# Two attentions in one kernel: the main loop's order and PSUM banks as one written list

## The chip, the core and the metric

The kernel runs on one core of a Trainium2 chip. The metric is the device time of the core in microseconds: 1790.12 us, the median of three runs (1788.89 to 1790.79). The engines that matter are TensorE (PE; its weight loads are shown as PEld), VectorE (DVE), ScalarE (ACT), GpSimd (POOL) and the DMA queue of SyncE (SP). Each engine runs its own instructions strictly in the order in which they stand, and waits where an operand is not ready.

## What is computed

Two multi-head attentions over 2048 rows of width 640 with 32 heads of 20 columns, in fp32; their outputs stand side by side.

```python
def _A_ref(x, wqkv, wo):            # local, dilated: 8 keys, 2 apart
    qkv = (x @ wqkv).reshape(B, S, 3, H, Dh).transpose(2, 0, 3, 1, 4)
    ...
    logits = jnp.einsum("bhsd,bhswd->bhsw", q, kg) * scale
    attn = _softmax(jnp.where(mask, logits, -1e9), axis=-1)
    o = jnp.einsum("bhsw,bhswd->bhsd", attn, vg)
    return o.transpose(0, 2, 1, 3).reshape(B, S, D) @ wo
def _B_ref(x, wqkv, wo):            # full attention
    scores = jnp.einsum("bhqd,bhkd->bhqk", q, k) * (Dh ** -0.5)
    o = jnp.einsum("bhqk,bhkd->bhqd", _softmax(scores), v)
    return o.transpose(0, 2, 1, 3).reshape(B, S, D) @ wo
return jnp.concatenate([a, b], axis=-1)
```

## The kernel before

Up to about 440 us the kernel projects q, k and v of both attentions. Then comes **the loop** over 512 steps of attention B. A step takes one block of 128 keys for one chunk of 512 queries and one group of four heads; 16 steps make a unit (one chunk), 64 a group. The last 24 steps run after the loop in a part of their own, which the change leaves alone, and then the rest of B's output projection follows.

Each step has three kinds of work for PE, and every product goes to a PSUM bank (there are eight, of 128 x 512 fp32) from which another engine must read it before PE may write there again:

- **S**, the scores: four halves, each one matmul `ps_st<-bq,bk` into one bank, read by one exp on ACT (`e<-ps_st`).
- **M**, the row maxima that a later step's exp needs: the scores of a block 24 steps ahead (`LEAD`) are made once more, four halves of one matmul `ps_st<-bk,bq` each, and DVE reads each with a maximum over its 512 columns (`mx<-ps_st`). Two halves in neighbouring banks can be read by one reduction of 1024 columns.
- **V**, the product of the exps of two steps ago (`LAG`) with the values: four matmuls `ps_st<-e,vb` side by side into one bank, which is kept over two steps, then copied out by ACT (`more<-ps_st`) and added up by POOL (`braw<-braw,more`).

The matmuls of one pair of halves run side by side in the array. In the same loop the rest of attention A runs: its scores and values on POOL (`akv`, `al`, `ao`), its softmax's maximum and reciprocal on DVE, and, for each of 16 tiles of 128 rows, five transposes on DVE (`turn<-ao`), a trip through DRAM, a split on POOL (`aot`) and two **out pieces** of 15 matmuls each on PE (`ps_st<-ww,aot`, `a_out`, line 480), each copied out by ACT (`ro<-ps_st`).

The order of all this is the order in which the Python code issues it: the wrapper `InOrder` (lines 48 to 62) records every instruction and keeps it there, so in the profile nearly all of them have line 61, and one goes by tile names. Two strings of letters set the loop's order (lines 984 and 985):

```python
PLAIN = "VYMSVYMSYY"
MIXED = "VYMSVYjMYYFYMSYVYMSVYSMYVYkYSVMSY"
```

V begins a step (`begin`, line 960, which also issues the DMAs, the POOL work and the short DVE jobs that are due) and issues the V product of two steps before. S is a pair of score halves, M a pair of maximum halves in two neighbouring banks with one reduction of 1024, Y one score half and one maximum half, whose reduction is one of 512. F is one out piece. j and k run short DVE jobs that wait in two lists, transposes among them (j: one softmax job or else three transposes; k: one softmax job and five transposes). MIXED is taken when an out piece is about to be ready, PLAIN otherwise.

The banks are reckoned while the code issues: `read_at` holds for each bank when it will have been read, by clocks that `InOrder` and `b_two` (line 779) keep for PE, ACT and DVE with fixed prices, and `one` and `two` (lines 139 and 145) take the bank, or the two neighbouring banks, that come free first.

Of the kernel before, what the change touches and what calls it, by code (L numbers as in the profile page):

```python
# [21 lines left out]
KC = 5  # L22
# [25 lines left out]
class InOrder:  # L48


    def __init__(self, tc, engine, fixed=0.0, rate=math.inf):
        self.tc, self.engine, self.fixed, self.rate = tc, engine, fixed, rate
        self.us = 0.0

    def __getattr__(self, name):
        op = getattr(self.engine, name)

        def emit(*a, us=None, **k):
            n = max([math.prod(x.shape[1:]) for x in a if hasattr(x, "shape")], default=0)
            self.us += self.fixed + n / self.rate if us is None else us  # L60
            return self.tc.keep_in_program_order(op(*a, **k))  # L61
        return emit


@with_exitstack
def attention_pair(ctx, tc, xa, wqk_a, wv_a, wo_a, xb, wqk_b, wv_b, wo_b, oa, ob):
# [5 lines left out]
    dr = ctx.enter_context(tc.tile_pool(name="dr", bufs=1, space=bass.MemoryType.DRAM))  # L72
    pe, gp, sp = (InOrder(tc, e) for e in (nc.tensor, nc.gpsimd, nc.sync))
    dve, act = InOrder(tc, nc.vector, 0.064, 960), InOrder(tc, nc.scalar, 0.111, 1400)

# [4 lines left out]
    def after(n, fn, *args):  # L80
        due.setdefault(now[0] + n, []).append((fn, args))

    loop = [None]

# [26 lines left out]
    taken = {}  # L111
    read_at = []

    def bank():

        if read_at:
            n = one(pe.us)
            pe.us = max(pe.us, read_at[n]) + 2.2
            act.us = max(act.us, pe.us + 0.05)
        else:  # L120
            n = free.pop(0)
        t = psb[:, n]
        taken[id(t)] = (n, t)
        return t

    def give(t):

        n = taken.pop(id(t))[0]
        if read_at:
            read_at[n] = act.us + 0.2  # L130
        else:
# [12 lines left out]

    def two(t):

        return min(range(7), key=lambda n: (max(t, read_at[n], read_at[n + 1]), abs(read_at[n] - read_at[n + 1])))

# [231 lines left out]
    def a_softmax(t):  # L380

        _, L, _ = a_t[t]
        if t % (NT // 2) == 0:
            pool(L, L, mask, ALU.add)
        yield
        if t < NT - 1:
            yield
        m = sb.tile([128, 4, H], F32, tag="am", bufs=2, name="am")
        job(soft_jobs, 0, lambda: dve.tensor_reduce(m[:, 0], L.rearrange("p o h -> p h o"), AX.X, ALU.max, us=0.53))
# [11 lines left out]
        job(soft_jobs, 0, lambda: dve.reciprocal(m[:, 0], m[:, 0], us=0.23))  # L401
        yield
        pool(L, L, m[:, 0].unsqueeze(1).to_broadcast([128, WIN, H]), ALU.mult)
# [210 lines left out]
    def max_rows(m4, m1, q, qc):  # L614
# [5 lines left out]
        def turn():  # L620

            dve.transpose(raw, m1, us=0.135)

# [19 lines left out]
    def normalize(raw, g, c0, t, gap, then):  # L643
# [15 lines left out]
        t = odd(t + gap)  # L659
        after(t, lambda: dve.reciprocal(sm, sm, us=0.157))  # L660
        after(t + 1, sp.dma_start, s_d[1].rearrange("j (p c) -> j p c", c=16), sm)
# [74 lines left out]

    exp_at = {}
    behind_v = [False]

    def b_pv(i):  # L740
        u, kb = divmod(i, NKB)
        g, qc = divmod(u, NQC)
        n, part = divmod(kb, 2)
        if read_at:
            t = max(pe.us + 0.12, exp_at.pop(i))
            if part == 0:
                o = one(t)
                accs[u] = o, psb[:, o]
                t = max(t, read_at[o])
                read_at[o] = 1e9  # L750
            pe.us = t + 0.866
            behind_v[0] = True
        elif part == 0:
            accs[u] = None, bank()
        o, acc = accs[u]
        for j in range(GH):
# [5 lines left out]
        del accs[u]  # L762
        act.us = max(act.us, pe.us + 0.322)
# [7 lines left out]
        if o is None:  # L771
            give(acc)
        else:
            read_at[o] = act.us + 0.25
        if kb == NKB - 1:
            last = g == NG - 1
            normalize(raws.pop(u), g, qc * 512, *((2, 3) if last else (5, 6)), (lambda: out_last(qc)) if last else None)

    def b_two(what):

        t = pe.us + 0.129 * behind_v[0]
        lag = 0.53 if behind_v[0] else 0.44
        both = what[0][0] == what[1][0] == "m"
        if both:
            n = two(t)
            ns, ts = (n, n + 1), [max(t, read_at[n], read_at[n + 1])] * 2
        else:
            ns, ts = [], []
            for _ in range(2):
                ns.append(one(max([t] + ts), *ns))  # L790
                ts.append(max([t] + ts + [read_at[ns[-1]]]))
        pe.us = ts[1] + (0.236 if ts[1] > ts[0] + 0.05 or (ts[0] < t + 0.02 and not behind_v[0]) else 0.336)
        behind_v[0] = False
        for (kind, *at), n in zip(what, ns):
            (s_matmul if kind == "s" else m_matmul)(*at, psb[:, n])
        for (kind, i, j, r), n, t in zip(what, ns, ts):
            if kind == "s":
                act.us = max(act.us, t + lag)
                s_exp(i, j, r, psb[:, n])
                exp_at[i] = act.us + 0.2  # L800
                read_at[n] = act.us + 0.18
            elif not both or r == 1:
                pq, ch = divmod(i % NKB, 2)
                m4 = mxt[i // NKB][0]
                dve.us = max(dve.us, t + lag)
                if both:
                    dve.tensor_reduce(m4[:, :, pq, 2 * ch + j], psb[:, ns[0]:ns[0] + 2], AX.X, ALU.max)
                    read_at[ns[0]] = dve.us + 0.13
                else:
                    dve.tensor_reduce(m4[:, r, pq, 2 * ch + j:2 * ch + j + 1], psb[:, n], AX.X, ALU.max)  # L810
                read_at[n] = dve.us + 0.13

    s_next, m_next, m_open, m_half = [0], [0], [None], set()

# [13 lines left out]
    def m_done(m):  # L828

        if m[1] in m_half:  # L830
            max_end(m[1])
        m_half.symmetric_difference_update({m[1]})

    def b_token(kind):

        m = None
        if kind == "S":
            what = [s_half(), s_half()]
        elif kind == "M":
            m = m_two()  # L840
            what = [(*m, 0), (*m, 1)]
        else:
# [7 lines left out]
        b_two(what)  # L850
        if m:
            m_done(m)
# [102 lines left out]
    loop[0] = now[0] + 1  # L955
    read_at += 8 * [0.0]
    for e in (pe, act, dve):
        e.us = 0.0

# [23 lines left out]

    PLAIN = "VYMSVYMSYY"
    MIXED = "VYMSVYjMYYFYMSYVYMSVYSMYVYkYSVMSY"
    i, order, mixed = 0, "", 0
    while i < NS - LEAD or order:
        if not order:
            if not left_a[0] and not WO_b:
                load_out(wo_b, WO_b)  # L990
            order = PLAIN
            if i + 6 <= NS - LEAD and ready_a and ready_a[0][0] <= now[0] + 3 and (
                    soft_jobs or next_a[0] == len(UNITS) or now[0] > max(mixed, ready_a[0][0]) + 14):
                order, mixed = MIXED, now[0] + 6
        kind, order = order[0], order[1:]
        if kind == "F":
            out_piece()
        elif kind == "j":
            run_jobs(*((soft_jobs, 1) if soft_jobs else (turn_jobs, 3)))
        elif kind == "k":  # L1000
            run_jobs(soft_jobs, 1)
            run_jobs(turn_jobs, KC)
        elif kind != "V":
            b_token(kind)
        else:
            begin(i)
# [9 lines left out]

    read_at.clear()
    for i in range(NS - LEAD, NS + LAG):
# [65 lines left out]
```

## Time and profile before

| what | us |
|---|---|
| median of three runs | 1790.12 (1788.89 to 1790.79) |
| span of the profiled execution | 1787.0 |
| median less that span | 3.1 |
| first exp of the loop starts | 440.0 |
| last maximum of the loop starts | 1669.6 |
| last exp starts | 1735.9 |

The profile is of one execution; its own time outside the span is not shown, so the span is set beside the median. The page gives each engine's busy time; a busy PE is one with a matmul in flight, not one at its full rate. Views by stretch ("windows") give the same for any part of the span, and a timeline gives the instructions in order, with the idle time of the engine before each in square brackets and what ended it. DVE and ACT overlap the end of one instruction with the start of the next, so in a run of equal instructions the busy time of the group divided by its count is less than the mean length of one.

### The profile page before, as it was taken

The numbers are of one execution on the slowest core, as the hardware profiler recorded it, in microseconds if no ns is written. First come the engines' busy times: TensorE is split into PE (matmuls) and PEld (weight loads), VectorE is DVE, ScalarE is ACT, GpSimd is POOL, SyncE is SP. The second block draws the span as 40 slices with busy tenths as digits, with TensorE's granted clock in tenths as the row PEclk, the third lists the DMA queues.
The fourth block names the chain that finished last, engine by engine and source line by source line (L and its number), as shares of the span: only waits on it lengthen the run. The fifth ranks groups of instructions, "written<-read, shape, count | busy, mean of one in ns | idle before, by whom it ended". The sixth has DMA issues, their size and how long they took to land. (4 is left out here: it accounts for less than half of the span.)

```text
span 1787.0 us, 31655 instructions
## 1 busy us (share of the span) xinstructions
PE 1772.1 (99%) x11211; PEld 987.1 (55%) x11211; DVE 1340.0 (75%) x1834; ACT 1327.2 (74%) x2593; POOL 1217.1 (68%) x1072
## 2 busy tenths in 40 slices
PE   9999999999999999999999999999999999999999
PEld 7988888887344444444444444444444434443469
DVE  3100232367999999999999999999999999999300
ACT  4222322222998999999999999998998998899881
POOL 0000069226679999989998999999999997337241
PEclk9999999999999999999999999999999999999999
DMA  6333696854535444354536336354444453113123
GB/s 228 116 100 102 190 304 245 270 187 139 152 88 148 124 136 120 106 151 133 147 99 170 96 113 163 121 159 130 133 142 124 122 149 94 30 44 86 32 70 114
DMA packets 191191, 240.22 MB, mean 134 GB/s; under 512 B 89020, under 2 KB 115260, under 8 KB 190040
## 3 DMA queue, kind: packets, MB, share of 16 engines
q1 hardware_dynamic: 190456, 237.54, 44.5%
q8 instruction: 88, 1.44, 0.4%
q14 instruction: 71, 0.58, 0.1%
q10 hardware_dynamic: 576, 0.66, 0.1%
HBM read 173.21 MB, written 64.91 MB: 133 GB/s over the span
## 5 line engine op out<-in xcount | busy, mean ns | idle before, releaser
L61 DVE TENSOR_REDUCE mx<-ps_st 128x1 f32<-128x512 f32 (+1 forms) x1512 | 1218.2, 871 | 57.7 <-PE ps_st L61 51.3
L61 ACT ACTIVATE e<-ps_st 128x512 f32<-128x512 f32 x2048 | 1066.2, 615 | 37.7 <-PE ps_st L61 16.4
L61 PE MATMUL ps_st<-bq,bk 62*128 62x512 f32 x2048 | 614.4, 436 | 1.4 <-DVE mx L61 0.6
L61 PE MATMUL ps_st<-bk,bq 60*128 60x512 f32 x2048 | 593.4, 446 | 3.9 <-DVE mx L61 2.1
L61 PEld LDWEIGHTS ps_st<-bq,bk 62*128 62x128 f32 x2048 | 283.0, 184 | 479.3 <-ACT e L61 282.3
L61 PE MATMUL ps_st<-e,vb 128*32 128x512 f32 x4096 | 543.7, 605 | 3.8 <-ACT e L61 2.6
L61 POOL TENSOR_TENSOR braw<-braw,more 128x512 f32<-128x512 f32 x224 | 287.8, 1285 | 136.5 <-ACT more L61 133.2
L61 POOL TENSOR_TENSOR akv<-akv,aq 128x1280 f32<-128x1280 f32 x64 | 189.0, 2953 | 234.4 <-DMA akv<-ka_d 234.4
L61 PEld LDWEIGHTS ps_st<-bk,bq 60*128 60x128 f32 x2048 | 267.7, 184 | 71.3 <-DVE mx L61 36.7
L61 POOL TENSOR_TENSOR akv<-akv 128x640 f32<-128x640 f32 (+3 forms) x304 | 282.2, 928 | 23.8
L61 ACT COPY ro<-ps_st 128x320 f32<-128x320 f32 (+2 forms) x124 | 61.2, 495 | 226.6 <-PE ps_st L61 177.2
L61 PEld LDWEIGHTS ps_st<-e,vb 128*32 128x32 f32 x4096 | 82.1, 108 | 158.8 <-ACT e L61 76.6
L61 POOL TENSOR_TENSOR akv<-akv,al 128x1280 f32<-128x1280 f32 x64 | 152.0, 2375 | 0.2
L61 ACT COPY more<-ps_st 128x512 f32<-128x512 f32 x224 | 133.4, 595 | 2.9 <-PE ps_st L61 2.7
L61 PE MATMUL ps_st<-wc,xn 128*128 128x512 f32 (+1 forms) x576 | 133.5, 376 | 0.4 <-ACT xn L61 0.4
L61 PE MATMUL ps_st<-ww,xn 128*128 128x320 f32 x768 | 125.8, 314 | 0.0
L61 PEld LDWEIGHTS ps_st<-ww,xn 128*128 128x128 f32 x768 | 113.4, 188 | 20.1 <-ACT ve L61 7.7
L61 PEld LDWEIGHTS ps_st<-wc,xn 128*128 128x128 f32 x576 | 106.2, 188 | 18.4 <-ACT xn L61 1.0
L61 PE MATMUL ps_st<-xn,w 128*128 128x512 f32 x480 | 115.7, 390 | 0.0
L61 PEld LDWEIGHTS ps_st<-xn,w 128*128 128x128 f32 x480 | 90.1, 188 | 19.4
L61 ACT CAST pr<-ps_st 128x512 fp32r<-128x512 f32 x40 | 23.5, 587 | 101.0 <-PE ps_st L61 101.0
L61 DVE TENSOR_TENSOR pr<-ps_st,pr 128x512 fp32r<-128x512 f32 x40 | 27.7, 692 | 91.7 <-ACT pr L61 91.7
(64 smaller groups left out, 986.0 us busy)
## 6 DMA issues: line engine op xcount, KB each, us to landing
akv<-ka_d SPq DMA_DIRECT2D x128, 320.0 KB
akv<-va_d SPq DMA_DIRECT2D x128, 320.0 KB
kb_d<-pr SPq DMA_DIRECT2D x20, 512.0 KB
qb_d<-pr SPq DMA_DIRECT2D x20, 512.0 KB
bk<-kb_d SPq DMA_DIRECT2D x16, 640.0 KB
bq<-qb_d SPq DMA_DIRECT2D x64, 160.0 KB
rb<-s_d SPq DMA_DIRECT2D x128, 64.0 KB
stg<-xb SPq DMA_DIRECT2D x12, 512.0 KB
```

The costliest lines, as they stand in the source:

```text
L61: return self.tc.keep_in_program_order(op(*a, **k))
```

## The change

Both strings, the clocks, `read_at`, `one` and `two` go. In their place stands `ORDER`, one string of some 6200 characters that lists every token of the loop, with the bank or banks that it writes. The letters mean what they meant, with these differences:

- V is followed by the bank that its product takes at every second step. F is followed by the bank of the out piece.
- S and Y are followed by two banks. M has one bank, the first of two neighbours, and one reduction of 1024.
- **N** is new: a pair of maximum halves in two banks of any place, read by two reductions of 512.
- j runs one transpose; k is gone. Softmax jobs run at the starts of steps only, as `begin` did before too.

The list holds 488 V, 32 F, 660 S, 632 Y, 509 M, 151 N and 80 j. The two strings came, over the loop, to 488 V, 32 F, 488 S, 976 Y and 488 M. The work is the same: 1952 score halves, 1952 maximum halves, 488 V products, 32 out pieces, 80 transposes. What moves is the order on PE, DVE and ACT, which bank each pair takes, and which maximum halves share a reduction. `m_done` now counts the halves of a unit, because halves of different steps can be open at once.

```diff
@@ InOrder
-    def __init__(self, tc, engine, fixed=0.0, rate=math.inf):
-        self.tc, self.engine, self.fixed, self.rate = tc, engine, fixed, rate
-        self.us = 0.0
+    def __init__(self, tc, engine):
+        self.tc, self.engine = tc, engine
...
+        return lambda *a, **k: self.tc.keep_in_program_order(op(*a, **k))
@@ bank, give
-        if read_at:
-            n = one(pe.us)
-            pe.us = max(pe.us, read_at[n]) + 2.2
-            act.us = max(act.us, pe.us + 0.05)
-        else:
-            n = free.pop(0)
+        n = given.pop(0) if given else free.pop(0)
...
-    def one(t, *but):
-
-        at = [1e9] + read_at + [1e9]
-        return min((n for n in range(8) if n not in but), key=lambda n: (
-            max(t, read_at[n]), -max(t, at[n]) - max(t, at[n + 2])))
...
@@ b_two
-    def b_two(what):
...
+    def b_two(what, ns, one):
+
         for (kind, *at), n in zip(what, ns):
             (s_matmul if kind == "s" else m_matmul)(*at, psb[:, n])
-        for (kind, i, j, r), n, t in zip(what, ns, ts):
+        for (kind, i, j, r), n in zip(what, ns):
             if kind == "s":
                 s_exp(i, j, r, psb[:, n])
-            elif not both or r == 1:
+            elif not one or r == 1:
...
+                if one:
+                    dve.tensor_reduce(m4[:, :, pq, 2 * ch + j], psb[:, n - 1:n + 1], AX.X, ALU.max)
                 else:
                     dve.tensor_reduce(m4[:, r, pq, 2 * ch + j:2 * ch + j + 1], psb[:, n], AX.X, ALU.max)
@@ the loop
-    PLAIN = "VYMSVYMSYY"
-    MIXED = "VYMSVYjMYYFYMSYVYMSVYSMYVYkYSVMSY"
-    i, order, mixed = 0, "", 0
-    while i < NS - LEAD or order:
...
+    ORDER = (
+        "Y07M1S36M4V0Y71M4M2S06V7Y06M2S14Y75V0Y16M2S74VY71M5S42S03N17V4Y05S61M2VY07M5S13S42N70V1Y36M4S72VY07M2S64S51N70"
...
+    for kind, *ns in re.findall("[A-Zj][0-7]*", ORDER):
+        ns = [int(n) for n in ns]
+        if kind == "j":
+            run_jobs(turn_jobs, 1)
+        elif kind not in "FV":
+            b_token(kind, ns)
+        else:
+            given += ns
+            if kind == "F":
+                out_piece()
+                continue
...
```

How the instructions move, at two places. First PE around the 13th out piece, where `bq,bk` is a score half, `bk,bq` a maximum half, `e,vb` a V product and `ww,aot` the piece. Before:

```order
L61 MATMUL ps_st<-bq,bk 128x512 x2
L61 MATMUL ps_st<-e,vb 32x512 x4
L61 MATMUL ps_st<-bq,bk 128x512
L61 MATMUL ps_st<-bk,bq 128x512 x3
L61 MATMUL ps_st<-bq,bk 128x512
L61 MATMUL ps_st<-bk,bq 128x512
L61 MATMUL ps_st<-bq,bk 128x512
L61 MATMUL ps_st<-bk,bq 128x512
L61 MATMUL ps_st<-ww,aot 128x320 x15
L61 MATMUL ps_st<-bq,bk 128x512
```

and now:

```order
L56 MATMUL ps_st<-e,vb 32x512 x4
L56 MATMUL ps_st<-bq,bk 128x512
L56 MATMUL ps_st<-bk,bq 128x512 x5
L56 MATMUL ps_st<-bq,bk 128x512 x2
L56 MATMUL ps_st<-ww,aot 128x320 x15
L56 MATMUL ps_st<-bq,bk 128x512
L56 MATMUL ps_st<-bk,bq 128x512 x3
L56 MATMUL ps_st<-bq,bk 128x512 x3
```

Before, the piece stood behind V, Y, M, Y, Y, so that the last two maximum halves before it came one by one, each beside a score half. Now it stands behind V, Y, M, M, S: the maximum halves come first, four of them in two neighbouring pairs, and the pair right before the piece is one of scores. The piece itself stands some 16 steps earlier in the loop than its counterpart did.

Second, DVE around the transposes of the seventh tile of A, where `mx<-ps_st 128x2` is a reduction of 1024 and `128x1` one of 512. Before:

```order
L61 TENSOR_REDUCE mx_8420<-ps_st 128x2
L61 TENSOR_REDUCE mx_8420<-ps_st 128x1
L61 TENSOR_REDUCE mx_8420<-ps_st 128x2
L61 TENSOR_REDUCE mx_8420<-ps_st 128x1 x2
L61 STREAM_TRANSPOSE turn<-ao 128x128 x5
L61 TENSOR_REDUCE mx_8420<-ps_st 128x1
L61 TENSOR_REDUCE mx_8420<-ps_st 128x2
L61 TENSOR_REDUCE mx_8420<-ps_st 128x1 x2
```

and now:

```order
L56 STREAM_TRANSPOSE turn<-ao 128x128
L56 TENSOR_REDUCE mx_7976<-ps_st 128x1
L56 TENSOR_REDUCE mx_7976<-ps_st 128x2
L56 TENSOR_REDUCE mx_8423<-ps_st 128x1 x5
L56 TENSOR_REDUCE mx_2486<-mx_7976 128x16
L56 STREAM_TRANSPOSE mtr<-mx_2486 128x32
L56 TENSOR_REDUCE mx_8423<-ps_st 128x2
L56 STREAM_TRANSPOSE turn<-ao 128x128
L56 TENSOR_REDUCE mx_8423<-ps_st 128x1
L56 STREAM_TRANSPOSE turn<-ao 128x128 x3
L56 TENSOR_REDUCE mx_8423<-ps_st 128x1
L56 TENSOR_REDUCE mx_8423<-ps_st 128x2
```

Before, the five transposes of a tile stood together, 16 steps behind the place where POOL's last addition to the tile is issued; now they are spread, the first 6 steps behind that place and the last 8. The five reductions of 512 in a row are those of N and Y tokens that follow each other.

More of the change, by code (lines that the diff above doesn't have):

```diff
@@ L1 @@
-import math
+import re
 from contextlib import ExitStack
@@ L48 @@
 class InOrder:
-    def __init__(self, tc, engine, fixed=0.0, rate=math.inf):
-        self.tc, self.engine, self.fixed, self.rate = tc, engine, fixed, rate
-        self.us = 0.0
+    def __init__(self, tc, engine):
+        self.tc, self.engine = tc, engine
     def __getattr__(self, name):
         op = getattr(self.engine, name)
[L58 to L62, printed above, removed]
+        return lambda *a, **k: self.tc.keep_in_program_order(op(*a, **k))
 @with_exitstack
@@ L72, in attention_pair @@
     dr = ctx.enter_context(tc.tile_pool(name="dr", bufs=1, space=bass.MemoryType.DRAM))
-    pe, gp, sp = (InOrder(tc, e) for e in (nc.tensor, nc.gpsimd, nc.sync))
-    dve, act = InOrder(tc, nc.vector, 0.064, 960), InOrder(tc, nc.scalar, 0.111, 1400)
+    pe, dve, act, gp, sp = (InOrder(tc, e) for e in (nc.tensor, nc.vector, nc.scalar, nc.gpsimd, nc.sync))
     now = [0]
@@ L81, in after @@
         due.setdefault(now[0] + n, []).append((fn, args))
-    loop = [None]
+    loop = [None, False]
     def odd(n):
@@ L111, in attention_pair @@
     taken = {}
-    read_at = []
+    given = []
     def bank():
-        if read_at:
-            n = one(pe.us)
-            pe.us = max(pe.us, read_at[n]) + 2.2
-            act.us = max(act.us, pe.us + 0.05)
-        else:
-            n = free.pop(0)
+        n = given.pop(0) if given else free.pop(0)
         t = psb[:, n]
-        taken[id(t)] = (n, t)
+        taken[id(t)] = (None if loop[0] is not None and loop[1] else n, t)
         return t
@@ L128, in give @@
         n = taken.pop(id(t))[0]
-        if read_at:
-            read_at[n] = act.us + 0.2
-        else:
+        if n is not None:
             free.append(n)
@@ L400, in a_softmax @@
         yield
-        job(soft_jobs, 0, lambda: dve.reciprocal(m[:, 0], m[:, 0], us=0.23))
+        job(soft_jobs, 0, lambda: dve.reciprocal(m[:, 0], m[:, 0]))
         yield
@@ L620, in turn @@
         def turn():
-            dve.transpose(raw, m1, us=0.135)
+            dve.transpose(raw, m1)
         def parts():
@@ L659, in normalize @@
         t = odd(t + gap)
-        after(t, lambda: dve.reciprocal(sm, sm, us=0.157))
+        after(t, dve.reciprocal, sm, sm)
         after(t + 1, sp.dma_start, s_d[1].rearrange("j (p c) -> j p c", c=16), sm)
@@ L743, in b_pv @@
         n, part = divmod(kb, 2)
[L744 to L755, printed above, removed]
+        if part == 0:
+            accs[u] = bank()
+        acc = accs[u]
         for j in range(GH):
@@ L770, in b_pv @@
             after(1, pool, raws[u], raws[u], more, ALU.add)
[L771 to L774, printed above, removed]
+        give(acc)
         if kb == NKB - 1:
@@ L777, in b_pv @@
             normalize(raws.pop(u), g, qc * 512, *((2, 3) if last else (5, 6)), (lambda: out_last(qc)) if last else None)
-    def b_two(what):
[L781 to L793, printed above, removed]
+    def b_two(what, ns, one):
         for (kind, *at), n in zip(what, ns):
             (s_matmul if kind == "s" else m_matmul)(*at, psb[:, n])
-        for (kind, i, j, r), n, t in zip(what, ns, ts):
+        for (kind, i, j, r), n in zip(what, ns):
             if kind == "s":
-                act.us = max(act.us, t + lag)
                 s_exp(i, j, r, psb[:, n])
-                exp_at[i] = act.us + 0.2
-                read_at[n] = act.us + 0.18
-            elif not both or r == 1:
+            elif not one or r == 1:
                 pq, ch = divmod(i % NKB, 2)
                 m4 = mxt[i // NKB][0]
[L805 to L808, printed above, removed]
+                if one:
+                    dve.tensor_reduce(m4[:, :, pq, 2 * ch + j], psb[:, n - 1:n + 1], AX.X, ALU.max)
                 else:
                     dve.tensor_reduce(m4[:, r, pq, 2 * ch + j:2 * ch + j + 1], psb[:, n], AX.X, ALU.max)
-                read_at[n] = dve.us + 0.13
-    s_next, m_next, m_open, m_half = [0], [0], [None], set()
+    s_next, m_next, m_open, m_left = [0], [0], [None], {}
     def s_half():
@@ L828, in m_done, with b_token @@
     def m_done(m):
[L830 to L834, printed above, removed]
+        u = m[1] // NKB
+        m_left[u] = m_left.get(u, 2 * (NKB - (LEAD % NKB if u == LEAD // NKB else 0))) - 1
+        if m_left[u] == 0:
+            max_end(u * NKB + NKB - 1)
+    def b_token(kind, ns):
         m = None
@@ L838, in b_token @@
             what = [s_half(), s_half()]
[L839 to L842, printed above, removed]
+        elif kind == "Y":
             o = s_half()
@@ L849, in b_token @@
                 what = [o, (*m, 1 - o[3])]
-        b_two(what)
+        else:
+            m = m_two()
+            what = [(*m, 0), (*m, 1)]
+        b_two(what, ns if len(ns) == 2 else (ns[0], ns[0] + 1), kind == "M")
         if m:
@@ L955, in attention_pair @@
     loop[0] = now[0] + 1
-    read_at += 8 * [0.0]
-    for e in (pe, act, dve):
-        e.us = 0.0
+    loop[1] = True
     def begin(i):
@@ L989, in attention_pair @@
+    i = 0
+    for kind, *ns in re.findall("[A-Zj][0-7]*", ORDER):
[4 more added lines that the diff above has]
+            b_token(kind, ns)
+        else:
+            given += ns
+            if kind == "F":
+                out_piece()
+                continue
             if not left_a[0] and not WO_b:
                 load_out(wo_b, WO_b)
[L991 to L1005, printed above, removed]
             begin(i)
@@ L1015, in attention_pair @@
             i += 1
-    read_at.clear()
+    loop[1] = False
     for i in range(NS - LEAD, NS + LAG):
```

65 lines of the change are left out of this document (58 added, 7 removed).

## The prediction

> **What bounds the kernel now.** I read the page first, then busy times by stretch, then who waits for whom, then one place in the timeline.
>
> ```profile
> PE 1772.1 (99%) x11211; PEld 987.1 (55%) x11211; DVE 1340.0 (75%) x1834; ACT 1327.2 (74%) x2593; POOL 1217.1 (68%) x1072
> L61 ACT ACTIVATE e<-ps_st x2048: 589/605/708, 440.0 to 1735.9; 128x512 f32<-128x512 f32 x187
> L61 DVE TENSOR_REDUCE mx<-ps_st x1512: 626/691/1241, 366.5 to 1669.6; 128x1 f32<-128x512 f32 x158, 128x2 f32<-128x1024 f32 x31
> ```
>
> The first line is of the page, the other two of the views by tile (count, shortest/median/longest in ns, first and last start). The page points to PE, at 99%. But the loop is what the change touches: from the first exp at 440.0 to the last maximum at 1669.6, some 1230 us. In that stretch (columns: length, then PE, PEld, DVE, ACT, POOL busy, then clock, DMA share and GB/s):
>
> ```profile
> 440.00:1670.00 1230.00, 1221.52 (x8288) 532.46 (x8284) 1195.79 (x1663) 1139.19 (x2244) 1060.08 (x921) 1.00 0.42 120
> ```
>
> DVE is busy 1195.8 of 1230 us, 97%, and ACT 93%. PE's 99% is no limit: its weight loads tell what it really does, which is to stand before banks that have not been read yet (waits from 475 to 1635 us):
>
> ```profile
> PEld ps_st L61 <- ACT e L61: 352.1, 609, 1.0
> PEld ps_st L61 <- DVE mx L61: 176.6, 356, 1.0
> ```
>
> That is 528.7 of 1160 us. So in the loop PE is paced by its readers, and DVE has the least room. The chain that ended last agrees: it runs through the maxima at the loop's end, and only then through PE for the last 24 steps and the projection, which the change does not touch:
>
> ```profile
> 1633.33 18.68 DVE mx L61 x24
> 1669.91 113.64 PE ps_st L61 x777
> ```
>
> What a better order can win is thus DVE's idle time in the loop, 1230 - 1195.8 = 34.2 us, and whatever changes in DVE's own work. Where does it sit idle? Busy time of DVE alone, in stretches chosen by the out pieces:
>
> ```profile
> 661.00:689.00 28.00, 27.96 (x39) 1.00 0.42 128
> 689.00:741.00 52.00, 50.14 (x72) 1.00 0.48 137
> 741.00:755.00 14.00, 13.96 (x21) 1.00 0.04 7
> 840.00:892.00 52.00, 50.33 (x73) 1.00 0.50 147
> 1500.00:1600.00 100.00, 99.88 (x694) 47.38 (x686) 92.62 (x129) 88.42 (x175) 35.18 (x34) 1.00 0.18 43
> ```
>
> Under PLAIN (first and third line) DVE is full: 27.96 of 28 and 13.96 of 14 us. Each stretch of two MIXED patterns with their two out pieces loses 1.86 and 1.67 us. There are 16 such pairs of pieces; 13 at about 1.77 make 23.0 us, and the last three lie in the last line, where DVE (third busy time) is idle for 7.4 us. Together 30.4 of the 34.2 us. One piece close up (timeline, columns: start, length, instruction, idle before it):
>
> ```profile
> 692.08 2.43 PE L61 MATMUL ps_st<-ww,aot 128*128 128x320 f32 x15
> 692.11 2.35 DVE L61 TENSOR_REDUCE mx<-ps_st 128x2 f32<-128x1024 f32 x3
> 694.44 0.50 PE L61 MATMUL ps_st<-bq,bk 62*128 62x512 f32 x1
> 694.54 0.42 ACT L61 COPY ro<-ps_st 128x320 f32<-128x320 f32 x1 [1.62 <-PE ps_st L61]
> 695.01 6.00 DVE L61 TENSOR_REDUCE mx<-ps_st 128x1 f32<-128x512 f32 x7 [0.55 <-PE ps_st L61]
> ```
>
> The piece holds PE for 694.44 - 692.08 = 2.36 us, and the first maximum fed after it starts 695.01 - 694.44 = 0.57 us after its matmul. DVE had work for 2.35 us when the piece began and then stood for 0.55. To lose nothing it must have 2.9 us in its queue at a piece.
>
> **The change part by part.** *DVE's own work.* The reductions by shape:
>
> ```profile
> L61 DVE TENSOR_REDUCE mx<-ps_st 128x2 f32<-128x1024 f32 x536 | 649.9, 1216 | 33.0 <-PE ps_st L61 32.8
> L61 DVE TENSOR_REDUCE mx<-ps_st 128x1 f32<-128x512 f32 x976 | 632.7, 681 | 24.7 <-PE ps_st L61 18.4
> ```
>
> Busy time over count is 1.212 us for a double and 0.648 for a single one. The list has 509 doubles for 488 and 632 + 2 x 151 = 934 singles for 976: +21 x 1.212 - 42 x 0.648 = -1.8 us. On the bound, so all of it counts.
>
> [...]
>
> *The out pieces.* From the order of both kernels I counted, for each of the 32 pieces, what DVE has to do between the last reduction whose bank PE must take back before the piece and the first reduction fed after it, at 1.212 and 0.648 us and the rows' times for short jobs. That is the most its queue can hold. Before, 24 of 32 pieces have 2.51 to 3.12 us (mean of all 3.13), so any wait of PE for ACT on the way leaves less than 2.9. In the list 28 have more than 3.2 us, the mean is 3.57, and one (2.94) is near the limit; 0.44 us more per piece. With 0.55 us at the piece above I put what all 32 lose now at 16 us, and let 2 remain: -14 us.
>
> *The rest of the mixed stretches.* 30.4 - 16 = 14.4 us are idle there away from the pieces, behind V products that follow too few maximum halves, as in MIXED's "kYSVMSY". The list has no fixed pattern there and orders each place by itself; since I cannot see how each turns out, I take half: -7 us, with 0 and -14 as bounds.
>
> *Overlap.* A single reduction shows 681 ns by itself but 648 in the group's busy time, so one that follows its predecessor at once hides part of itself. Some 60 waits (the next line) end with a reduction that does not. Without most of them: -2 us, bounds 0 and -5.
>
> ```profile
> DVE mx L61 <- PE ps_st L61: 26.1, 59, 1.5
> ```
>
> *What costs nothing.* Clocks and bank choice are Python; no instruction is in them. Out pieces stand up to 30 steps earlier, ACT's copy and the store with them; the exps around hide them as now. The same 80 transposes are spread one by one; same busy time.
>
> Sum: -1.8 - 14 - 7 - 2 = -24.8, say -25 us. Span 1787.0 - 25 = 1762; with the 3.1 us by which the median lies above the span, **1765 us**. Bounds of the unknown terms, everything working together: -1.8 - 34.2 - 5 = -41 (1749); only the pieces: -16 (1774).
>
> What binds next at -25 us? ACT has 91 us of room. POOL is nearer, since A's work fills it until about 1500 us:
>
> ```profile
> 600.00:1500.00 900.00, 894.88 (x6074) 390.48 (x6074) 877.44 (x1227) 834.24 (x1644) 853.70 (x736) 1.00 0.46 132
> ```
>
> Its 853.7 of 900 us leave 46 us; of the 25 some 18 fall into this stretch, so POOL goes to 97%, not over.
>
> **Rivals.**
>
> *Everything closes up.* DVE never starves, span 1746, median 1749. For it: PLAIN stretches do run full. Against: 488 V products and 32 pieces would all have to fit.
>
> *The idle time moves.* The list packs maximum halves ahead of pieces, so the tokens beside have fewer, and DVE loses under the plain steps what it gains at pieces; within 3.6 us of now, **1790**. For it: PLAIN's 99.9% has nothing to give and any new pattern there can only lose. Against: the count of queued work rises at the pieces without a like fall elsewhere.
>
> *Banks that fit the list's clock and not the chip's.* PE stands in order, so a bank that is read late holds everything behind it, the feed of DVE included. A maximum half that takes back a bank from DVE itself is safe only if DVE has more to do than the 0.57 us from matmul to reduction, and behind a V product more than that product too:
>
> ```profile
> 695.62 1.06 PE L61 MATMUL ps_st<-e,vb 128*32 128x512 f32 x8
> 696.62 0.50 PE L61 MATMUL ps_st<-bq,bk 62*128 62x512 f32 x1
> ```
>
> That is 1.00 us, 1.57 together. By the order, halves with at most 1.25 us of DVE work in between go from 146 to 270. If the 124 more stand behind V products or waits for ACT and lose 0.3 us each, 37 us, the sum turns to +12: **1802**. It decides once the mean loss exceeds 25/124 = 0.2 us. For it: the 528.7 us of waits above show that PE arrives late at banks as a rule. Against: most of those 124 need no V in between, and 0.65 us then cover 0.57.
>
> *Transposes too early.* They stand 5 to 9 steps (once 2) behind POOL's last addition instead of mostly 16; should POOL fall further behind than 5 steps (12 us at 2.4 us a step), DVE, the bound, waits for it at each of the 16 tiles. At 95 to 97% load POOL's queue can grow. Two to three us each would be +40, with the sum +15: **1805**. In the stretch above an addition to `braw` runs about 5 us behind the copy that feeds it, which leaves 7:
>
> ```profile
> 690.86 0.59 ACT L61 COPY more<-ps_st 128x512 f32<-128x512 f32 x1
> 696.09 1.28 POOL L61 TENSOR_TENSOR braw<-braw,more 128x512 f32<-128x512 f32 x1
> ```
>
> **How the numbers follow.** Forecast (a gain of 12 to 38 us) 0.62; everything closes up 0.08; the idle time moves 0.15, of which half still ends a little faster; banks 0.10; transposes 0.05. The forecast's own range is 1752 to 1778. For 8 in 10 I go to 1748 below, which takes in half of the best case, and to 1789 above, which takes in most of the case in which idle time moves; the two slow rivals stay out. 0.2% of the time, 3.6 us, is about what a measurement of this kernel tells from no change. Faster by more: 0.62 + 0.08 + 0.08 = 0.78; within: 0.07; slower: 0.15.
>
> **What would show it.** DVE's idle time between the first exp and the last maximum should fall from 34 to about 12 us, and that stretch from 1230 to about 1205, while what lies before and after keeps its length. ACT's wait for `ro` (1.62 us at a piece) stays, DVE's [0.55 <-PE] behind pieces goes. Reductions: 557 doubles, 934 singles. Wrong it would be if DVE's busy share falls, if waits of DVE for PE appear in stretches without a piece, or if `turn<-ao` shows a wait for POOL.

## The result and the profile after

The changed kernel takes 1791.36 us (median of 20 runs, 1789.03 to 1794.73), the kernel before on the same chip 1788.8 us (20 runs). The ratio is 1.0018, with a 95% interval of 1.0011 to 1.0025: no gain, but a small loss of 2.6 us. The span of the profiled execution is 1789.2 us (before 1787.0; the execution itself took 1791.02).

The first exp of the loop starts 2.5 us earlier than before (437.5), the last maximum 3.4 us later (1673.0). First the same stretch that the prediction used, then a piece of it in which the difference sits, each in the changed kernel (views by stretch):

```profile
440.00:1670.00 1230.00, 1213.39 (x8282) 542.35 (x8280) 1190.73 (x1637) 1133.67 (x2235) 1058.28 (x920) 0.99 0.42 120
500.00:600.00 100.00, 92.38 (x624) 40.73 (x620) 89.66 (x124) 85.94 (x170) 84.44 (x73) 0.95 0.41 119
```

The kernel before had 98.43 us of DVE work in the second stretch, and a granted clock of 1.00 in both. To compare the two fairly I take a point that both reach alike, 400 us, and go to the start of the last maximum. First line before, second line after (DVE alone):

```profile
400.00:1669.60 1269.60, 1226.78 (x1692) 1.00 0.42 121
400.00:1673.00 1273.00, 1225.75 (x1671) 0.99 0.42 121
```

DVE works 1.0 us less and is idle for 4.4 us more. Each idle piece of DVE runs from the end of all that was issued to the next start. I sorted these pieces by length and place; "at an out piece" means that the next instruction starts between 0.3 us before and 1.3 us after ACT begins to copy that piece:

| DVE idle, us | before | after |
|---|---|---|
| at the 32 out pieces | 13.7 | 9.8 |
| elsewhere, waits under 0.75 us | 26.8 | 19.4 |
| elsewhere, waits of 0.75 us and more | 2.3 (2 waits) | 18.1 (7 waits) |

So the written order is better where it was written to be better, by 3.9 + 7.4 us of idle time at the pieces and in short waits and 1.0 us of work, and gives back 15.8 us in seven long ones. Three places hold nearly all of these: 7.3 and 1.6 us at 566 to 569 us, 1.6 and 1.4 at 1207 to 1209, 3.3 and 0.8 at 1446 to 1451; the seventh is 2.1 us at the loop's start. The view of PE's own waits names the cause of the first two, that of DVE's waits the third (columns: total, count, longest):

```profile
PE ps_st L56 <- DMA bq<-mdr: 9.9, 2, 7.4
PE ps_st L56 <- DVE mx L56: 3.6, 4, 2.9
DVE am L56 <- POOL al L56: 3.3, 1, 3.3
```

In the kernel before PE never waited for `bq<-mdr`. This is the last link of a chain that the prediction did not look at. When DVE has reduced a unit's maxima, it transposes them (`mtr`), POOL splits them in two parts, SP stores them to DRAM (`mdr<-mtr`) and loads them into the spare rows of `bq`, and only then may PE make the first scores of that unit. The split on POOL, for unit 3 (timeline of POOL, changed kernel; DVE's transpose had ended at 545.3):

```profile
551.75 2.93 POOL L56 TENSOR_TENSOR akv<-akv,aq 128x1280 f32<-128x1280 f32 x1
554.75 3.43 POOL L56 TENSOR_TENSOR akv<-akv 128x640 f32<-128x640 f32 x4
558.26 0.32 POOL L56 TENSOR_TENSOR al<-akv 128x64 f32<-128x64 f32 x1
558.52 0.21 POOL L56 CAST mtr<-mtr 128x32 fp32r<-128x32 f32 x1
558.81 0.25 POOL L56 TENSOR_TENSOR mtr<-mtr 128x32 fp32r<-128x32 f32 x1
```

and what follows on SP, PE and DVE:

```profile
559.09 1.74 SPq L56 DMA_DIRECT2D mdr<-mtr  x4
562.86 0.53 SPq L56 DMA_DIRECT2D bq<-mdr  x2
564.57 1.05 PE L56 MATMUL ps_st<-bq,bk 62*128 62x512 f32 x2 [7.39 <-DMA bq<-mdr]
565.80 1.29 DVE L56 TENSOR_REDUCE mx<-ps_st 128x1 f32<-128x512 f32 x2 [7.31 <-PE ps_st L56]
568.71 2.05 DVE L56 TENSOR_REDUCE mx<-ps_st 128x1 f32<-128x512 f32 x3 [1.62 <-PE ps_st L56]
```

The split takes 0.54 us of work and comes out 13.8 us after the transpose, because two units of A's work stand ahead of it on POOL, one running and one more. In the kernel before only the running one did (timeline, with the load on SP and the unit's first scores on PE):

```profile
546.80 0.32 POOL L61 TENSOR_TENSOR al<-akv 128x64 f32<-128x64 f32 x1
547.08 1.29 POOL L61 TENSOR_TENSOR braw<-braw,more 128x512 f32<-128x512 f32 x1
548.31 0.21 POOL L61 CAST mtr<-mtr 128x32 fp32r<-128x32 f32 x1
...
552.75 0.54 SPq L61 DMA_DIRECT2D bq<-mdr  x2
...
558.62 0.50 PE L61 MATMUL ps_st<-bq,bk 62*128 62x512 f32 x1
```

Counted from step 0, the list completes unit 3's maxima in step 41 instead of 39 and begins its scores in step 47 instead of 48. A's units on POOL are issued at fixed steps, so the two steps put one more of them ahead of the split. PE then stops for 7.39 us, and does not come back at full speed. Views by stretch around the stop (the last three numbers are the granted clock, the DMA share and GB/s):

```profile
556.00:559.00 3.00, 1.18 (x10) 0.67 (x6) 2.45 (x3) 2.35 (x5) 2.61 (x7) 1.00 0.00 0
559.00:562.40 3.40, 0.00 (x0) 0.00 (x0) 0.00 (x0) 0.00 (x0) 3.32 (x4) 0.50 0.09 24
562.40:565.80 3.40, 1.23 (x4) 0.79 (x4) 0.00 (x1) 0.43 (x1) 3.32 (x3) 0.50 0.62 175
565.80:569.20 3.40, 3.40 (x15) 1.03 (x14) 1.78 (x3) 1.18 (x4) 2.21 (x2) 0.50 0.97 197
569.20:572.60 3.40, 3.39 (x26) 1.18 (x24) 3.17 (x5) 3.10 (x8) 1.32 (x2) 0.99 0.61 222
```

In the second of these PE, DVE and ACT run nothing: the maximum halves that stand behind the waiting scores on PE do not pass them and begin at 565.14, though DVE had stood idle since 558.5. In the fourth PE is busy throughout and gets through 15 matmuls; in the fifth through 26. The eight matmuls of V products take 1.93 us in the fourth (from 565.98) and 1.06 in the fifth (from 569.36). The 1.62 us wait of DVE before 568.71 lies in the slow stretch.

### The profile page after: what moved, and what is told of

Same layout as the page of the kernel before. It is cut to its first block, busy times and chain, and to the rows that moved or that the text cites. A ratio compares the mean times of both kernels' runs of the same rounds, so it can differ in the third digit from the quotient of the medians.

```text
span 1789.2 us, 31500 instructions
## 1 busy us (share of the span) xinstructions
PE 1764.0 (99%) x11211; PEld 996.0 (56%) x11211; DVE 1338.1 (75%) x1813; ACT 1326.4 (74%) x2593; POOL 1216.7 (68%) x1072
## 4 chain that ended last, share of the span: by engine, by line
PE 84%; DVE 5%; POOL 5%; ACT 2%; DMA 2%; issue 1%; SPq 1%; POOLq 0%; ACTq 0%; DVEq 0%
PE ps_st L56 84%; DVE mx L56 5%; POOL akv L56 3%; ACT e L56 2%; POOL braw L56 1%; SPq L56 1%; DMA bk<-kb_d 1%; DMA vb_d<-ve 0%; DMA s_d<-sm 0%; DMA akv<-ka_d 0%; POOL ao L56 0%; ACT more L56 0%; POOL al L56 0%; DMA back<-tr_d 0%; DMA bq<-mdr 0%
## 5 line engine op out<-in xcount | busy, mean ns | idle before, releaser
L56 PE MATMUL ps_st<-bq,bk 62*128 62x512 f32 x2048 | 557.3, 440 | 11.5 <-DMA bq<-mdr 9.9
L56 PE MATMUL ps_st<-bk,bq 60*128 60x512 f32 x2048 | 539.9, 441 | 6.4 <-DVE mx L56 4.5
L56 PEld LDWEIGHTS ps_st<-bq,bk 62*128 62x128 f32 x2048 | 278.9, 185 | 460.9 <-ACT e L56 276.6
L56 POOL TENSOR_TENSOR braw<-braw,more 128x512 f32<-128x512 f32 x224 | 287.7, 1284 | 133.4 <-ACT more L56 122.8
L56 PEld LDWEIGHTS ps_st<-bk,bq 60*128 60x128 f32 x2048 | 249.4, 185 | 88.5 <-DVE mx L56 56.4
L56 PEld LDWEIGHTS ps_st<-xn,w 128*128 128x128 f32 x480 | 90.1, 188 | 19.4
```

The costliest lines, as they stand in the source:

```text
L56: return lambda *a, **k: self.tc.keep_in_program_order(op(*a, **k))
```

## The experiments

The runs were timed on four chips, each time beside the kernel before, which took 1788.26, 1789.84, 1790.71 and 1790.1 us there. The ratios are to that time on the same chip; a difference from the changed kernel's 1791.36 us is uncertain by some 2 us.

**The list's tokens with reckoned banks.** The list's order, with each V, S, Y, M, N and F in its place, but without its digits: `one`, `two` and `read_at` choose the banks as in the kernel before; then the same with N read by one reduction of 1024 in two neighbouring banks.

```diff
-        b_two(what, ns if len(ns) == 2 else (ns[0], ns[0] + 1), kind == "M")
+        b_two(what, kind == "M")
```

and for the second kernel:

```diff
-    for kind in re.sub("[^A-Zj]", "", ORDER):
+    for kind in re.sub("[^A-Zj]", "", ORDER).replace("N", "M"):
```

> The list's tokens in the list's order, but the banks reckoned while issuing, as the kernel before does. Theory A (the order makes the gain and the late loads the loss): within 6 us of the changed kernel, 1786 to 1797 us, and the wait for the maxima of unit 3 is still there. Theory B (the written banks are what costs): at least 10 us faster than the changed kernel, 1781 us or less. A third way (the written banks carry the gain): more than 8 us slower than the changed kernel.

> As the run with reckoned banks, but every N is issued as M: neighbouring banks and one reduction of 1024, 151 times. By the rows DVE has 12.7 us less to do. If DVE's work is the bound, 8 to 13 us faster than the run with reckoned banks alone. If waiting for two neighbouring banks at once costs PE and DVE more than the second reduction, equal or slower.

Measured: 1810.8 us (ratio to the kernel before 1.0123, 1.0109 to 1.0138) and 1888.85 us (1.0557, 1.0542 to 1.0571). The first is the third way of its expectation. DVE's short waits away from the pieces are 36.0 us in it, for 19.4 in the list, while its long ones are fewer (12.5 us for 18.1); its work is 4.4 us more (1230.1 us from 400 us to the last maximum, for 1225.75). So for this order the written banks are worth 19 us over reckoned ones (1810.8 - 1791.4), most of it in short waits. The second result shows what N is for. PE's waits for a bank in the loop, first the list with reckoned banks, then the same with N as M:

```profile
PE ps_st L62 <- ACT e L62: 9.3, 27, 0.7
PE ps_st L62 <- DVE mx L62: 4.4, 12, 1.1
```

```profile
PE ps_st L62 <- ACT e L62: 48.3, 80, 1.1
PE ps_st L62 <- DVE mx L62: 13.1, 18, 1.2
```

In the list as written the first of these waits is 0.7 us. A pair in two neighbouring banks must wait until both of them are free, and the waits that grow most, from 9.3 to 48.3 us, are for a bank that ACT still has to read; N takes any two. Two reductions of 512 cost DVE 84 ns more than one of 1024 by the rows of the prediction (2 x 0.648 - 1.212 us), 12.7 us for 151 of them. Not having them costs 78 us (1888.85 - 1810.8) on reckoned banks, and the 12.7 us do not even show: up to the last maximum DVE's work is 1238.0 us, 7.9 more than with N, and its idle time 133.4 us for 60.6.

**Maxima before the piece, in the old pattern.** One change to the kernel before, which puts two whole maximum pairs and a score pair ahead of an out piece, as the list does:

```diff
-    MIXED = "VYMSVYjMYYFYMSYVYMSVYSMYVYkYSVMSY"
+    MIXED = "VYMSVYjMMSFYMSYVYMSVYSMYVYkYSVMSY"
```

> The kernel before with one edit: in MIXED the two Y ahead of the out piece become M and S (the same halves, maxima first, scores last). 32 more double and 64 fewer single reductions are 2.7 us less DVE work. Theory A (DVE starves at the pieces because its queue there is short): its idle time at the pieces falls by 8 to 14 us and the kernel takes 1773 to 1781 us. Theory B (idle time only moves): ACT gets its two score halves late, PE waits for its banks, and the time stays within 4 us of 1789.

Measured: 1789.88 us, ratio 1.0006 (0.9998 to 1.0015). DVE's idle time at the pieces is 15.9 us here, not less than the 13.7 before, so theory A fails in its mechanism too. From 400 us to the last maximum DVE works 2.2 us less (1224.6 for 1226.8) and is idle for 4.1 us more (46.9 for 42.8). Writing only the place beside the piece anew thus turns saved work into idle time, near to the rival "the idle time moves", though the pieces gain nothing here.

**Units 3 and 19 split off POOL.** In the changed kernel, for these two units only:

```diff
+        late = u in (3, 19)
+
         def parts():
+            if late:
+                act.copy(mt[:, 1], raw)
+                after(1, dve.tensor_tensor, mt[:, 2], raw, mt[:, 1].bitcast(F32), ALU.subtract)
+                return
             gp.tensor_copy(mt[:, 1], raw)
             gp.tensor_tensor(mt[:, 2], raw, mt[:, 1].bitcast(F32), ALU.subtract)
```

> The changed kernel, but the split of the row maxima of units 3 and 19 is done by ACT (cast) and DVE (subtraction) instead of POOL, so that it does not stand in POOL's queue. Theory A (the list gains about 25 us, and a few late inputs take it back: the maxima of unit 3 and of unit 19 leave POOL 13 and 9 us after DVE made them, PE stands 7.4 and 2.5 us for their load and runs at half clock for 10.2 and 3.4 us afterwards): both waits vanish and the clock stays full there, 10 to 17 us faster than the changed kernel, 1774 to 1781 us. Theory B (the list gains nothing as such, its banks do not fit the chip, and time saved in one place is lost in the next): at most 5 us faster, 1786 us or more.

Measured: 1784.82 us, ratio 0.9977 (0.9967 to 0.9986), 6.5 us less than the changed kernel. That is between the two expectations: PE no longer waits for unit 3's load, but still 2.0 us for that of unit 19, and DVE's wait for `al` is still there (3.0 us). (The 10.2 us at half clock in the expectation hold the stop itself, from 559.0 on; after the restart it was 4.6 us.) The run also pays for its own means: DVE's subtraction of 128x32 for unit 3 takes 2.22 us, from 552.36 to 554.58, where that for unit 19 takes 0.15, and it ends just after a product of POOL (`akv<-akv,aq`, 551.59 to 554.53) that it overlaps. Whether POOL held it up was not tried. PE then waits 1.85 us for DVE (before 556.37). These 2 us of DVE make the gain a little too small a measure of what the stop costs.

**A late load in the kernel before.** The other way round: the stop alone, in the kernel that has none. The additions are work that the kernel does not need.

```diff
         def parts():
+            if u == 3:
+                z = sb.tile([128, 128], F32, name="held")
+                gp.memset(z, 0.0)
+                for _ in range(20):
+                    gp.tensor_tensor(z, z, z, ALU.add)
             gp.tensor_copy(mt[:, 1], raw)
```

> The kernel before, with some 7 to 9 us of needless additions on GpSimd right ahead of the split of unit 3's row maxima, so that their way through DRAM ends late for the first scores of unit 3, as it does in the changed kernel. Theory A (one late load stops TensorE, its clock then drops, and VectorE never makes it up): the granted clock shows a dip as in the changed kernel, VectorE stands for 2 to 6 us there, and the time rises by 3 to 8 us, to 1791 to 1797. Theory B (the loop has room to make up one such stop later): the time is within 1.5 us of the kernel before.

Measured: 1795.08 us, ratio 1.0031 (1.002 to 1.0043): 5.2 us slower. The timeline of DVE at the place, and the clock in the stretch that follows:

```profile
565.86 1.82 DVE L61 TENSOR_REDUCE mx<-ps_st 128x1 f32<-128x512 f32 x2 [4.51 <-PE ps_st L61]
568.98 3.61 DVE L61 TENSOR_REDUCE mx<-ps_st 128x1 f32<-128x512 f32 x5 [1.30 <-PE ps_st L61]
```

```profile
566.00:570.00 4.00, 4.00 (x22) 1.26 (x18) 2.70 (x4) 2.95 (x6) 3.69 (x6) 0.71 0.67 205
```

The waits are 4.51 + 1.30 = 5.8 us, and the loss 5.2: one late small load goes into the time almost in full (1795.08 for 1789.84 on the same chip), and the loop does not make it up.

**A held back for the split.** In the changed kernel no unit of A is issued when a split is due at the next step (`splits` holds the steps at which they are due), and the softmax job of A's last tile comes two steps later. No work is added.

```diff
-        if i > 14 and (i % 30 % 4 == 1 if i < 240 else i % 14 in (1, 5, 7, 11)):
+        if i > 14 and ((i % 30 % 4 == 1 if i < 240 else i % 14 in (1, 5, 7, 11)) and i != 397 or i == 401):
+            owed[0] += 1
+        if owed[0] and now[0] + 1 not in splits:
+            owed[0] -= 1
             run_jobs(soft_jobs, 2)
```

> The changed kernel, but a unit of A's work on GpSimd is held back for one step wherever the split of a unit's row maxima is due at the next step, so that the split stands ahead of it on GpSimd, and the softmax job of A's last tile comes two steps later. No work is added or removed. Theory A (the written order is about 12 us better in its short waits, and the long waits behind GpSimd, 7.4 us at the scores of unit 3, 2.5 us at unit 19 and 3.3 us at the reduction of al, take it back): these waits go, VectorE's waits of 0.75 us and more between 400 us and the last maximum fall from 19.8 to under 8 us, and the time is 1775 to 1781 us. Theory B (GpSimd is late as a whole, and what is early at one unit is late at the next): the long waits turn up at other units, and the time is 1784 us or more.

The same hold in the kernel before, without the change at step 397:

> The kernel before, with A's units on GpSimd held back for the split of the maxima as in the run on the changed kernel. Same work. Theory A (the hold helps the changed kernel only because its loads came late; the kernel before has no load that TensorE waits for): within 2 us of the kernel before. Theory B (the hold is good by itself, so that it says nothing of the list): 3 us or more faster.

Measured: 1784.54 us (0.9972, 0.9962 to 0.9983), and in the kernel before 1793.59 us (1.0016, 1.0007 to 1.0025). The hold as such is thus no gain: in the kernel before it costs 2.9 us, outside both theories. DVE waits 5.2 us for `al` at 1442 there, presumably since the unit of A that writes `al` is held back too; in the list the hold takes some 7 us off, together with the move at step 397. The first run comes out at the time of theory B, but not by its mechanism: no new unit is late. The same three places still wait, only shorter (2.2 us at unit 3, 2.0 at unit 19, 1.75 behind `al`), and DVE's long waits fall to 12.4 us instead of 8:

```profile
PE ps_st L56 <- DMA bq<-mdr: 4.2, 2, 2.2
PE ps_st L56 <- DVE mx L56: 2.3, 3, 1.8
```

**Later scores.** The remaining two stops are a matter of 2 us each, so in addition the first scores of units 3 and 19 go one V product further back, against maximum halves:

```diff
-    S76 N40 V1 Y72 S35 N46
+    N76 N40 V1 Y72 S35 S46
...
-    Y32 V0 S17 j M4 Y63
+    N32 V0 Y17 j S45 Y63
```

In this first run of it the three units of A around the last softmax were moved further back as well (steps 400, 402 and 403).

> As the run that holds A's work back for the split, and besides: at units 3 and 19 two tokens each change places, so that the unit's first score halves come about one V product later and maximum halves stand where they were, and the softmax job of A's last tile comes one or two steps later still. Same work. Theory A (the remaining waits of 2.2, 2.0 and 1.8 us on TensorE and the reduced clock behind them are all that stands between that run and the list's full gain): VectorE's waits of 0.75 us and more fall from 12.4 to 6 us or less, and the time is 1774 to 1781 us. Theory B (an order written for fixed times yields new late places as soon as it runs faster): the time is within 2 us of 1784.5.

Measured: 1782.62 us (0.996, 0.9946 to 0.9973), theory B by the number, just (within 2 us of 1784.5). PE's stops at units 3 and 19 shrink to 0.51 and 0.66 us, but a new wait has come, on ACT, and it comes from the later softmax:

```profile
1452.26 0.42 ACT L56 ACTIVATE al<-al 128x256 f32<-128x256 f32 x1 [6.23 <-POOL al L56]
```

Where DVE no longer waits for `al`, ACT does; PE and then DVE (6.2 us at 1454) stand behind it. So two more runs, both with nothing held from step 385 on: one with the three units at 400, 403 and 405, one with A's units there as in the changed kernel.

> As the run with the hold and the later scores, but near the end of A (steps 385 on) nothing is held, and the three units around the last tile's softmax come at steps 400, 403 and 405 instead of 397, 399 and 403, so that neither VectorE's reduction of al nor ScalarE's exp of al should stand before GpSimd. Theory A (in the run before it the 6.2 us wait at 1453 us came from the shift of the softmax job alone, since ScalarE stood before GpSimd's al; without it the list shows its full gain): VectorE's waits of 0.75 us and more are 6 us or less in sum, and the time is 1774 to 1779 us. Theory B (each late place removed makes the next): another wait of 2 us or more turns up, and the time stays at 1781 us or more.

> As the run with the hold and the later scores, but with A's units at their places of the changed kernel from step 385 on. Theory A: the late loads of units 3 and 19 are gone and the wait of 3.3 us for al at 1446 us is back as in the changed kernel, so the time is 1777 to 1781 us. Theory B: another wait of 2 us or more turns up elsewhere, and the time is 1782 us or more.

Measured: 1779.82 us (1776.85 to 1780.31; 0.9936, 0.9924 to 0.9949) and 1781.57 us (0.9958, 0.9944 to 0.9972). The second lies between its two theories. In it DVE stands for 5.8 us before `al`, not the 3.3 expected; that DVE now comes there earlier while POOL's queue is as long would explain it, and was not tried by itself. The first is 10 us and more below both kernels. From 400 us to its last maximum (DVE alone), and PE's waits in the loop:

```profile
400.00:1661.80 1261.80, 1227.06 (x1672) 1.00 0.43 122
```

```profile
PE ps_st L56 <- DMA bq<-mdr: 2.3, 4, 1.2
PE ps_st L56 <- ACT e L56: 1.8, 3, 1.4
PE ps_st L56 <- DVE mx L56: 1.6, 4, 0.9
```

The last maximum starts 7.8 us earlier than before. DVE's waits of 0.75 us and more, pieces included, are 7.8 us in sum where the changed kernel had 19.8, and theory A wanted 6 or less; the short ones are 26.9, much as in the changed kernel (27.5). So the list's better short waits and the long waits are two separate things, and the first stays when the second is taken away. The 1779.82 lies just above theory A's range and below theory B's. What is left near A's end is 0.9 and 1.5 us at 1442 to 1446, behind the 1.2 us in the first line: PE now waits there for the load of unit 25, which it did not in the changed kernel. With A's units at their old places that wait is absent, so it came from my shift of them.

## Why the prediction was wrong

It said 1765 us, from four terms that make 25 us; the range reached to 1789. The time is 1791.36. One of its own signs of being wrong came true: DVE waits for PE where there is no piece, 7.31 us before 565.80.

*DVE's own work, -1.8 us.* It fell by 1.0 us, with the counts as told. Each instruction counted from the end of the one before it, from 400 us to the last maximum, the reductions fed by PE take 1.8 us less, as forecast, and the transposes, put at the same busy time, 0.7 us more (16.6 for 15.9). The busy time of the transposes as a group grows by 3.0 us, but that is mostly because those that stood together overlapped each other (221 ns of busy time each, for a mean length of 277), and now overlap the reductions beside them (259 for 287):

```profile
L56 DVE STREAM_TRANSPOSE turn<-ao 128x128 f32<-128x128 f32 x80 | 20.7, 287 | 0.0
L61 DVE STREAM_TRANSPOSE turn<-ao 128x128 f32<-128x128 f32 x80 | 17.7, 277 | 0.0
```

*The out pieces, -14 us.* They gave 3.9. The size failed on both sides. What all 32 lose was taken from one piece at 0.55 us; in the trace of before the first piece of a pair mostly loses 0.5 to 0.6 us, but the second of each of the first 13 pairs at most 0.21, once 0.36, and the 32 lose 13.7, not 16. And the count of the work that DVE can have queued (28 pieces above 3.2 us, against 2.9 needed) is the most that it can have: in the trace of after DVE still runs dry 2.1 to 2.8 us after the start of 23 of the pieces, less than the 2.9 needed, and the mean loss over all is 0.31 us (before 0.43). The queue is rarely as full as the order allows.

*The rest of the mixed stretches, -7.* Short waits elsewhere fell by 7.4 us: right in size.

*Overlap, -2.* It rested on most of some 60 waits going away. The view that counted 59 of them counts 50 in the changed kernel, so the condition was not met, and with the 1.8 us above explained by the counts alone nothing of this term shows.

*What costs nothing* is the step that failed and turned the sign: it put at nothing what measured 15.8 us of long waits. It named clocks, banks, out pieces and transposes, and passed over what moves with them: the step at which each unit's maxima are complete and that at which its scores begin. For POOL the prediction had only asked whether its 95% of load would pass 100%. The load did not matter. What mattered was the order within POOL's queue: a split of 0.5 us that stands behind 7 us more of A's work, at a place where before there was little room: SP issued the load at 552.75, and PE began the unit's scores at 558.6, where 1.7 us lie between the two when PE waits (562.86 to 564.57), so some 4 us to spare. The split off POOL and the hold of A shorten these stops by two independent means, later scores shorten them further, and each of these runs is 6.5 us or more faster than the list as written; the late load in the kernel before makes that slower by 5.2. Of the 18.1 us of long waits 16.0 sit at units 3 and 19 and at the last tile's softmax; the other 2.1 are at the loop's start, where the kernel before waits for 1.5.

*The rivals.* "The idle time moves" named the time, 1790, by luck and not by its way: idle time did not go from the pieces to the steps beside them, since short waits fall at both, and the loss is in seven long waits. "Banks that fit the list's clock" is not what happened: short waits fall with the written banks, and with the old reckoning in place of the written banks the same order takes 19 us more and its short waits nearly double. "Transposes too early" had the right engine, POOL's queue, and the wrong instruction: DVE never waits for `ao` in the loop; it waits for `al` once, and PE for the split twice.

With most of these waits gone the list gains 10.3 us (1790.1 to 1779.82), so that the 25 us would have been more than twice the gain even then. The part that was mis-sized is the out pieces, by 10 us.

## What to carry to other kernels

When an order is written anew, list for each chain that leaves the engine under study and comes back (here DVE, POOL, DRAM, PE) when it must be back and how much room it had, and see what now stands ahead of it in the queues that it passes. The busy share of an engine off the bound says little about this; with POOL busy for 853.7 and for 855.3 of 900 us, the split of 0.54 us came out 8.5 us after its input before (540.4 to 548.9) and 13.8 us after it now, by what was issued just ahead of it. And a loss seen at one place is not the loss at all places of its kind: look at them all before multiplying.

## What the runs showed of the hardware

In this kernel a stop of PE costs DVE more than itself: for the 7.39 us at unit 3 DVE stood for 7.31 + 1.62 = 8.9 us, and for the 4.38 us that PE waited in the kernel before with the late load 4.51 + 1.30 = 5.8 us. After the 7.39 us the granted clock was 0.50 up to about 569.2, some 4.6 us past the restart; in the kernel before it was 1.00 from 558 to 570. The clock also was lower behind shorter stops: in the changed kernel PE had waited for 2.53 us up to 1206.34, and the clock was then 0.57 over 4 us; in the run with A held it had waited for 1.75 us up to 1441.46:

```profile
1207.00:1211.00 4.00, 4.00 (x22) 1.03 (x14) 2.59 (x5) 2.08 (x4) 3.69 (x6) 0.57 0.32 122
```

```profile
1441.00:1445.00 4.00, 3.54 (x14) 1.32 (x16) 2.82 (x5) 0.68 (x3) 3.84 (x5) 0.53 0.26 71
```

A wait of 2.0 us (4.2 - 2.2, for unit 19's load) that ended at about 1199.6, in the same run, left it at 1.00:

```profile
1199.00:1203.00 4.00, 3.42 (x26) 1.11 (x26) 2.21 (x5) 2.06 (x4) 3.92 (x3) 1.00 0.47 166
```

So in these runs the length of a single wait does not tell whether the clock falls. PE also stands before banks in short waits throughout this loop (its weight loads for 528.7 of 1160 us in the kernel before, 1.0 us at the longest); whether they count as well, no run here separates.
